# Two F blocks of a SwiGLU down projection: a plain pair, or part of a two-pair Strassen group

## Chip, cores and metric

One Trainium2 chip, one of its cores. The metric is device time in microseconds of one execution, median of three runs before the change.

## The reference

A token block of 2048 x 576 is normalised; a linear-attention branch gives `s`, a SwiGLU feed-forward branch gives `g`, and the result is `x + s * silu(g)`. Cut to what matters here:

```python
def _B_ref(x, w_gate, w_up, w_down):      # F = 4608
    g = _silu(x @ w_gate)
    u = x @ w_up
    return (g * u) @ w_down

xn = _layernorm(x, axis=-1)
s = _A_ref(xn, A_wqkv, A_w_phi, A_wo)     # linear attention, heads of 18
g = _silu(_B_ref(xn, B_w_gate, B_w_up, B_w_down))
return x + s * g
```

So there is a SiLU inside the feed-forward branch (after `w_gate`) and a second one, the gate, on its finished result. The change touches the second.

## The kernel before

**Number format.** Every fp32 operand is split into a high and a low part (`split`, L57: ScalarE copies the high part, VectorE subtracts it to get the low one), and a product is three matmuls: high x high, high x low, low x high (`three`, L665, for the down projection).

**Stages.** Attention first, up to some 500 us. Then the feed-forward branch in two token halves, i = 0 and i = 1, of 1024 tokens each (eight tiles of 128). F is cut into 36 blocks of 128. A *unit* (i, n, f) is one F block f of one half, at place n = 0 to 35 in the half's order (L828 to L833). Six F blocks per half were computed early and lie in DRAM (`stored`, L583); the other units are *gate/up* units (`gate_up`, L591), which multiply the normalised tokens by a block of `w_gate` and `w_up` in a seven-product Strassen scheme and leave h, 128 x 1024, as two tiles `ha` and `hb` of 128 x 512. One product is seven matmuls of 128 x 512 (`product`, L566) into the PSUM tiles px (two buffers), pw and py. Between products ScalarE copies px out (`snap`, L596 to L600) before the next product accumulates into it.

**Down projection.** Two consecutive units make a pair; in pairs, h times `w_down` is a 2 x 2 block product: two token quarters by two F blocks by two column halves of 288. `strassen` (L730) computes it with seven products p1 to p7. Each product has a `prep` (differences on POOL at L753 to L779, then `split_h`, L578, and a split of the 128 x 288 weight block) and two `item`s (L785), each 2 x 3 matmuls of 128 x 288 per pair of the group into one PSUM tile pd (two buffers), followed by one eviction of 128 x 576: a VectorE addition into a running sum at L794 (a ScalarE copy, L792, for the first group of a half). A group normally holds two pairs (four units): the same eviction then serves both pairs. The running sums are `acc[:, 0]` to `acc[:, 3]` (C11, C12, C21, C22), P1 and P6 in the SBUF slot X02, and P7 in `sx`. `combine` (L811), in two parts, adds P1, P6 and P7 into the four C blocks, with POOL and VectorE instructions of 128 x 1152.

36 units are nine times four. Before, the last four units of each half are taken apart: units 32 and 33 are a group of a single pair, then comes `combine`, and units 34 and 35 are a `plain` pair (L672): for each of eight token tiles ScalarE copies the combined `acc` into pd (L690), 24 matmuls add both F blocks of the pair, and the result leaves PSUM. In the first half it leaves through the gate's SiLU back into `acc` (L698) and a 288 KB write to `y_dram`, issued from ScalarE (L699); in the second half `finish` (L637) multiplies it by `s`, adds `x` and writes the output.

**Order.** The down projection's steps go into a Python list, `queue`. `fill` (L846) is called four times in each unit (in a gate/up unit after the second, fourth, fifth and seventh product; four times in a row in a stored unit) and emits items until their cost reaches `share`: 2 up to n = 30, 3 from n = 31 (RUSH). An item costs the number of its pairs, a plain tile 2; `fill` stops when 3 cost units (LAG) or less are left. `look` (L836) runs the prep of the steps soon due. `combine`'s parts are put in ahead of p2 and p3 and behind them (L900 to L903). With the queue's rules followed by hand, the items fall like this around the border between the halves (x2 and x1: pairs in the group; T0 to T7: plain tiles):

```
i=0 n=32  p7 p4 | p4 p5 | p5 p6 | p6 p2   all x2
    n=33  p2 p3 x2 | p3 x2, p1 x1 | - | -
    n=34  p1 p7 p7 | p4 p4 p5 | p5 p6 p6 | combine0 p2   all x1
    n=35  - | - | - | -
i=1 n=0   p2 p3 x1 | p3 x1, combine1, T0 | T1 | T2     (stored)
    n=1   T3 | T4 | T5 | T6
    n=2   - | - | - | -
    n=3   T7 | p1 | p1 | p7   x2, first group of the second half
```

The emitted program is then ordered for each engine by a list scheduler with its own cost model, in which px copies, SiLUs and additions of `gate_up` have high priority; so items may move some way from their call. All engines run their own queue in order. SP issues the loads and stores: at the border seven X tiles of the second half (L514 to L530, each into the slot that the last unit of the first half frees), then the stored h (L586), weights (L546, L555), `w_down` rows (rt, rb at L727; for a plain pair ld at L679) and the loads of `late_finish` (L645), which turns `y_dram` of the first half into output during the second.

Of the kernel before, what the change touches and what calls it, by code (L numbers as in the profile page):

```python
# [11 lines left out]
AF = mybir.ActivationFunctionType  # L12
# [9 lines left out]
HT = HS // P  # L22
NF = F // P
HALF = D // 2
# [22 lines left out]
def gated_hedgehog_kernel(ctx: ExitStack, tc, x, w_qk, w_v, w_phi, wo, w_gu, w_tail, w_down, ident_in, mask_in, out):  # L47
# [5 lines left out]
    nc = tc.nc  # L53
# [3 lines left out]
    def split(hi, lo, src):  # L57
        nc.scalar.copy(hi, src)  # L58
        nc.vector.tensor_sub(lo, src, hi)  # L59
# [17 lines left out]
    y_dram = dram.tile([HT, P, 2, HALF], F32, name="y_dram")  # L77
# [431 lines left out]
    acc = fp.tile([P, 4, HT // 2, HALF], F32, name="acc")  # L509

    def operands(i):

        xo = [None] * 7
        for n in (0, 6, 1, 3, 5, 2, 4):  # L514
            if n < 3:
                j = (0, 1, 3)[n]
                if i:
                    t = xpool.tile([P, 5, BT], F32R, name=f"X0{j}")
                    nc.sync.dma_start(t.bitcast(F32), a_dram[n])
                else:  # L520
                    t = XB[0][j]
                xo[n] = [t[:, c] for c in range(5)]
                continue
            j = n - 3
            t = xpool.tile([P, 5, BT], F32R, name=f"X1{j}")
            nc.sync.dma_start(t.bitcast(F32).rearrange("p c n -> p (c n)"),
                              sum_dram[i, :, j].rearrange("p s c n -> p (s c n)"))
            v = t.rearrange("p c n -> p (c n)").rearrange("p (s c n) -> p s c n", s=4, c=5)
            xo[n] = [v[:, :, c] for c in range(5)]
        return xo  # L530
# [47 lines left out]
    def split_h(src):  # L578
        t = fp.tile([P, 2, BT], F32R, name="hh", bufs=4)
        split(t[:, 0], t[:, 1], src)  # L580
        return t

    def stored(src, fill):  # L583
        h = h_tile()
        for r in range(2):
            nc.sync.dma_start(h[r], src[:, r * BT:(r + 1) * BT])  # L586
        for _ in range(4):
            fill()
        return h
# [47 lines left out]
    def finish(t, k, pd, sx, eng):  # L637
        r0 = HS + t * P
        a = acc[:, t // 4 * 2:t // 4 * 2 + 2, t % 4][:, k]
        nc.scalar.activation(a, pd, AF.Silu)  # L640
        nc.vector.tensor_mul(a, a, halves_of(sx[:, 0])[:, k])  # L641
        eng.tensor_add(a, a, halves_of(sx[:, 1])[:, k])
        nc.sync.dma_start(halves_of(of[r0:r0 + P, :])[:, k], a)

    def late_finish(t):  # L645

        y = fw.tile([P, D], F32, name="ts")
        sx = fw.tile([P, 2, D], F32, name="ld", bufs=2)
        r = slice(t * P, t * P + P)
        nc.sync.dma_start(halves_of(y), y_dram[t])  # L650
        for m, src in enumerate((s_dram, xf)):
            nc.sync.dma_start(sx[:, m], src[r, :])
        nc.vector.tensor_mul(y, y, sx[:, 0])
        nc.vector.tensor_add(y, y, sx[:, 1])
        nc.sync.dma_start(of[r, :], y)

    def final_rows(n):
        name = ("X02", "X00", "X01", "X03")[3 - n]
        t = xpool.tile([P, 2, 2, D], F32, name=name)
        r = slice(HS + 2 * n * P, HS + 2 * n * P + 2 * P)  # L660
        for m, src in enumerate((s_dram, xf)):
            nc.sync.dma_start(t[:, :, m], src[r, :].rearrange("(a p) n -> p a n", p=P))
        return t

    def three(ps, hs, ws, first):  # L665
        for n, (h, w) in enumerate((a, b) for b, a in zip(ws, hs)):
            mm = ((h[0], w[0]), (h[0], w[1]), (h[1], w[0]))
            for m, (l, r) in enumerate(mm):
                nc.tensor.matmul(ps, l, r, start=first and n == 0 and m == 0, stop=n == len(hs) - 1 and m == 2,  # L669
                                 skip_group_check=True)  # L670

    def plain(i, fs, hr, final):  # L672

        ws = []

        def weights():
            raw = fw.tile([P, 2, D], F32, name="ld", bufs=2)
            for n, f in enumerate(fs):
                nc.sync.dma_start(raw[:, n], w_down[f * P:(f + 1) * P, :])  # L679
            for n in range(2):  # L680
                w = fq.tile([P, 2, D], F32R, name="dw", bufs=3)
                split(w[:, 0], w[:, 1], raw[:, n])
                ws.append(w)

        def tile_of(t, hs):
            pd = fps.tile([P, 2, 512], F32, name="pd", bufs=2)
            fine = i == 1 and t == HT // 2 - 1
            c = slice(t % 4 * P, t % 4 * P + P)
            a2 = acc[:, t // 4 * 2:t // 4 * 2 + 2, t % 4]
            nc.scalar.copy(pd[:, :, 0:HALF], a2)  # L690
            for k in range(2):
                n = slice(k * HALF, (k + 1) * HALF)
                three(pd[:, k, 0:HALF], [(h[:, 0, c], h[:, 1, c]) for h in hs], [(w[:, 0, n], w[:, 1, n]) for w in ws],
                      False)
                if fine:
                    finish(t, k, pd[:, k, 0:HALF], final[t // 2][:, t % 2], nc.vector)
            if i == 0:
                nc.scalar.activation(a2, pd[:, :, 0:HALF], AF.Silu)  # L698
                nc.scalar.dma_start(y_dram[t], a2)  # L699
            elif not fine:  # L700
                finish(t, slice(0, 2), pd[:, :, 0:HALF], final[t // 2][:, t % 2], (nc.vector, nc.gpsimd)[t % 2])

        for r in (1, 0) if i else (0, 1):
            hs = []

            def prep(r=r, hs=hs):
                if not ws:
                    weights()
                hs += [split_h(hr[n][r]) for n in range(2)]

            queue.append([2, prep, [(2, lambda t=4 * r + t, hs=hs: tile_of(t, hs)) for t in range(4)]])
# [3 lines left out]
    def pair_sums(i):  # L715
        if (i, 0) not in extra:
            extra[i, 0] = xpool.tile([P, 2, HT // 2, HALF], F32, name="X02")
        return extra[i, 0]

    def last_sum(i):  # L720
        if (i, 1) not in extra:
            extra[i, 1] = fp.tile([P, HT // 2, HALF], F32, name="sx")
        return extra[i, 1]
# [87 lines left out]
    def combine(i, part, final):  # L811
        P1, P6, P7 = pair_sums(i)[:, 0], pair_sums(i)[:, 1], last_sum(i)
        C11, C12, C21, C22 = (acc[:, n] for n in range(4))
        if part == 0:
            nc.vector.tensor_add(P6, P6, P1)
            nc.vector.tensor_add(P7, P7, P6)
            nc.gpsimd.tensor_add(P6, P6, C22)
            nc.vector.tensor_sub(C21, P7, C21)
            nc.vector.tensor_add(C22, C22, P7)
            for k in (3, 2)[0:2 * i]:  # L820
                final[k] = final_rows(k)
        else:
            nc.gpsimd.tensor_add(C11, C11, P1)
            nc.vector.tensor_add(C12, C12, P6)
            for k in (1, 0)[0:2 * i]:
                final[k] = final_rows(k)

# [41 lines left out]
    finals, late = {}, list(range(HT))  # L869
    for i, n, f in units:  # L870
        share[0] = 2 if n < RUSH else 3
        if i == 1 and n == 0:
            xo = operands(1)
        if f >= EARLY:
            w = kept.pop() if i and kept else ready.pop(0)
            if (i, f) == (0, NF - 1):
                kept.append(w)
            if todo and (i, f) != (0, NF - 1):
                ready.append(gate_up_weights(*todo.pop(0)))
        h = stored(h_dram[i, f], fill) if f < EARLY else gate_up(w, xo, fill, (i, f) == (0, EARLY))  # L880
        if n % 2 == 0:
            g = {"f": (f, units[units.index((i, n, f)) + 1][2]), "h": [h]}
            if n % 4 == 0:
                group = []
            if n < NF - 2:
                group.append(g)
        else:
            g["h"].append(h)
        if n >= NF - 2:
            if n % 2:  # L890
                plain(i, g["f"], g["h"], finals)
            continue
        if n >= NF - 4 or n % 4 > 1:
            strassen(i, group, n % 2, n < 4)
        if n % 2 == 0:
            continue
        if i and n >= 15 and late:
            with tc.issue_after(anchor[-1].ins):
                late_finish(late.pop(0))
        if n == NF - 3:  # L900
            for k in range(2):
                queue.insert(len(queue) - 2 + 3 * k,
                             [0, None, [(0, lambda i=i, k=k: combine(i, k, finals))]])  # L903
# [37 lines left out]
```

## Time and profile before

| | |
|---|---|
| median of three runs | 1654.41 us (1653.33 to 1656.06) |
| profiled execution | 1654.66 us, of it span 1652.9 us |
| granted TensorE clock | 0.999 |
| down matmuls (pd, 128 x 288) | 3048 |
| first half's units | from about 546 us to about 1087 us |
| second half's units | from there to about 1593 us, then a tail without gate/up products |
| VectorE, ScalarE, POOL busy | 71%, 43%, 38% of the span |
| DMA queue of SP | 44.9% of the 16 engines' time |

How to read it: a matmul's length in the trace is that of one alone; they overlap, so the distance between the starts of two groups, divided by the count, is the price of one. Idle time of an engine other than TensorE costs nothing unless TensorE ends up waiting. A row of the timeline gives start, length, engine, line, operation, output and input tiles, count, and in brackets idle time before it and what ended that. In the tables of waits the line in front is the waiter.

### The profile page before, as it was taken

To read this page: it belongs to the slowest core of one execution; us is meant where nothing else is said; L and a number is where in the kernel's file an instruction comes from. 1 tells how busy PE (TensorE), PEld (TensorE's weight loads), DVE (VectorE), ACT (ScalarE), POOL (GpSimd) and SP (SyncE) were. 2 spreads that over 40 slices of the span, in tenths; PEclk is the share of its full clock that TensorE was granted. 3 is DMA by queue.
4 is the path that set the end of the run, shared out by engine and by line. 5 is a ranking of instruction groups with operands and counts; after the bars stand their busy time and mean duration, and the time that the engine had idled before them with its cause. 6 is when DMAs were issued, how large, how long until landed. Compare 5 with 4: busy or idle time off the path is not lost.

```text
span 1652.9 us, 25205 instructions
## 1 busy us (share of the span) xinstructions
PE 1614.8 (98%) x9441; PEld 1434.1 (87%) x9441; DVE 1175.4 (71%) x1722; ACT 715.7 (43%) x1389; POOL 622.1 (38%) x660
## 2 busy tenths in 40 slices
PE   6999999999999999999999999999999999999998
PEld 5899998999987688888888888888888888888887
DVE  7678758899852477887787777845567667566578
ACT  5533345444431455445444444445433333433334
POOL 3467500343202444554554453422333234133132
PEclk9999999999999999999999999999999999999999
DMA  8623313343218545445445444495444556556435
GB/s 284 215 77 109 109 34 111 94 141 109 73 47 306 182 159 190 158 167 186 161 171 185 174 173 165 132 355 185 152 137 148 164 182 202 171 178 194 139 114 172
DMA packets 118108, 264.69 MB, mean 160 GB/s; under 512 B 12418, under 2 KB 48386, under 8 KB 116194
## 3 DMA queue, kind: packets, MB, share of 16 engines
q1 hardware_dynamic: 107628, 247.44, 44.9%
q0 software_dynamic: 3072, 11.02, 2.4%
q10 hardware_dynamic: 7286, 4.63, 0.9%
q8 instruction: 74, 1.21, 0.3%
q14 instruction: 48, 0.39, 0.1%
HBM read 164.21 MB, written 98.83 MB: 159 GB/s over the span
## 4 chain that ended last, share of the span: by engine, by line
PE 64%; DVE 3%; DMA 1%; issue 1%; POOL 0%; ACT 0%; SPq 0%; DVEq 0%; POOLq 0%
PE px L570 23%; PE pd L669 22%; PE pw L570 11%; PE py L570 6%; PE pe L92 2%; DVE hh L59 1%; DMA ha<-h_dram 1%; DVE acc L641 0%; DVE dw L59 0%; DVE acc L794 0%; DMA X<-s_dram 0%; DMA rb<-in_B_w_down 0%; DVE w L59 0%; DVE X L794 0%; DVE ha L630 0%
## 5 line engine op out<-in xcount | busy, mean ns | idle before, releaser
L669 PEld LDWEIGHTS pd<-dw,hh 128*128 128x128 f32 x3048 | 430.9, 188 | 31.6 <-DVE dw L59 6.4
L669 PE MATMUL pd<-dw,hh 128*128 128x288 f32 x3048 | 448.0, 297 | 8.4 <-DVE dw L59 4.8
L570 PE MATMUL px<-X,w 128*128 128x512 f32 x1440 | 374.8, 394 | 1.8 <-ACT w L58 1.0
L570 PEld LDWEIGHTS px<-X,w 128*128 128x128 f32 x1440 | 261.4, 188 | 55.9 <-ACT s L599 6.1
L570 PE MATMUL pw<-X,w 128*128 128x512 f32 x720 | 186.7, 394 | 0.0
L570 PEld LDWEIGHTS pw<-X,w 128*128 128x128 f32 x720 | 134.0, 189 | 30.2 <-DVE s L604 0.3
L604 DVE TENSOR_TENSOR s<-pw,s 128x512 f32<-128x512 f32 x120 | 82.8, 690 | 105.2 <-ACT s L599 93.4
L92 PE MATMUL pe<-X,wh 128*128 128x512 f32 (+1 forms) x480 | 152.0, 400 | 1.7 <-POOL X L199 0.7
L794 DVE TENSOR_TENSOR acc<-pd,acc 128x576 f32<-128x576 f32 x128 | 96.1, 752 | 72.2 <-PE pd L669 72.0
L599 ACT COPY s<-px 128x512 f32<-128x512 f32 x120 | 70.3, 586 | 156.4 <-PE px L570 156.3
L59 DVE TENSOR_TENSOR hh<-ha,hh 128x512 fp32r<-128x512 f32 x140 | 110.6, 815 | 23.6 <-ACT hh L58 23.0
L58 ACT CAST hh<-ha 128x512 fp32r<-128x512 f32 x140 | 83.1, 620 | 97.2 <-PE pd L669 79.9
L92 PE MATMUL p<-KVWH,X 128*128 128x288 f32 (+1 forms) x640 | 123.6, 298 | 0.9 <-DVE phi L274 0.9
L92 PEld LDWEIGHTS pe<-X,wh 128*128 128x128 f32 (+1 forms) x480 | 88.5, 189 | 19.7 <-DVE h L120 1.5
L766 POOL TENSOR_TENSOR hb<-hb 128x512 f32<-128x512 f32 x34 | 46.1, 1355 | 152.3 <-DVE hb L626 151.8
L92 PEld LDWEIGHTS p<-KVWH,X 128*128 128x128 f32 (+1 forms) x640 | 100.5, 188 | 1.7 <-issue 1.3
L59 DVE TENSOR_TENSOR w<-ld,w 128x512 fp32r<-128x512 f32 (+1 forms) x90 | 76.3, 848 | 34.2 <-ACT w L58 33.2
L753 POOL TENSOR_TENSOR h<-ha,hb 128x512 f32<-128x512 f32 x34 | 45.7, 1344 | 142.6 <-DVE ha L630 101.1
L570 PE MATMUL px<-X,wt 96*128 96x512 f32 x240 | 94.8, 395 | 0.0
L570 PE MATMUL py<-X,w 128*128 128x512 f32 x360 | 93.7, 394 | 0.1
L58 ACT CAST w<-ld 128x512 fp32r<-128x512 f32 (+1 forms) x90 | 49.4, 549 | 83.5 <-POOL ld L560 50.8
L779 POOL TENSOR_TENSOR ha<-ha 128x512 f32<-128x512 f32 x34 | 52.3, 1554 | 80.5 <-DVE hh L59 80.5
(181 smaller groups left out, 3046.9 us busy)
## 6 DMA issues: line engine op xcount, KB each, us to landing
w_dram<-w SPq DMA_DIRECT2D x87, 512.0 KB, 2.8
w<-w_dram SPq DMA_DIRECT2D x87, 512.0 KB, 4.5
wt<-t_dram SPq DMA_DIRECT2D x59, 336.0 KB, 3.4
ld<-in_B_w_gu SPq DMA_DIRECT2D x30, 512.0 KB, 4.4
X<-sum_dram SPq DMA_DIRECT2D x8, 1280.0 KB, 6.6
rt<-in_B_w_down SPq DMA_DIRECT2D x33, 288.0 KB, 3.2
rb<-in_B_w_down SPq DMA_DIRECT2D x33, 288.0 KB, 3.4
w_dram<-w SPq DMA_DIRECT2D x29, 256.0 KB
```

What stands on the lines that cost most here:

```text
L58: nc.scalar.copy(hi, src)
L59: nc.vector.tensor_sub(lo, src, hi)
L92: nc.tensor.matmul(ps, l, r, start=n == 0, stop=n == len(pairs) - 1)
L570: nc.tensor.matmul(ps, l, r, start=first and n == 0, stop=last and n == len(mm) - 1, skip_group_check=True)
L599: nc.scalar.copy(t, ps)
L604: nc.vector.tensor_add(t, ps, t)
L669: nc.tensor.matmul(ps, l, r, start=first and n == 0 and m == 0, stop=n == len(hs) - 1 and m == 2, skip_group_check=True)
L753: sub(s, g["h"][0][0], g["h"][0][1])
L766: nc.gpsimd.tensor_add(a21, a21, g["h"][1][1])
L779: sub(a12, a12, g["h"][0][0])
L794: nc.vector.tensor_add(a2, pd[:, :, 0:HALF], a2)
```

## The change

In the first half the last four units form one ordinary two-pair group, like the eight groups before it; `plain` stays for the second half only. `combine` of the first half comes after that group, and each of its parts ends with the gate: for each of the two C blocks that it has finished, one SiLU of 128 x 1152 in place on `acc` and one write into `y_dram`, issued from ScalarE (two C blocks hold the same four token tiles, one column half each). The second half's grouping is the same as before.

```diff
--- before.py
+++ after.py
@@ -669,7 +669,7 @@
                 nc.tensor.matmul(ps, l, r, start=first and n == 0 and m == 0, stop=n == len(hs) - 1 and m == 2,
                                  skip_group_check=True)
 
-    def plain(i, fs, hr, final):
+    def plain(fs, hr, final):
 
         ws = []
 
@@ -684,7 +684,7 @@
 
         def tile_of(t, hs):
             pd = fps.tile([P, 2, 512], F32, name="pd", bufs=2)
-            fine = i == 1 and t == HT // 2 - 1
+            fine = t == HT // 2 - 1
             c = slice(t % 4 * P, t % 4 * P + P)
             a2 = acc[:, t // 4 * 2:t // 4 * 2 + 2, t % 4]
             nc.scalar.copy(pd[:, :, 0:HALF], a2)
@@ -694,13 +694,10 @@
                       False)
                 if fine:
                     finish(t, k, pd[:, k, 0:HALF], final[t // 2][:, t % 2], nc.vector)
-            if i == 0:
-                nc.scalar.activation(a2, pd[:, :, 0:HALF], AF.Silu)
-                nc.scalar.dma_start(y_dram[t], a2)
-            elif not fine:
+            if not fine:
                 finish(t, slice(0, 2), pd[:, :, 0:HALF], final[t // 2][:, t % 2], (nc.vector, nc.gpsimd)[t % 2])
 
-        for r in (1, 0) if i else (0, 1):
+        for r in (1, 0):
             hs = []
 
             def prep(r=r, hs=hs):
@@ -811,17 +808,28 @@
     def combine(i, part, final):
         P1, P6, P7 = pair_sums(i)[:, 0], pair_sums(i)[:, 1], last_sum(i)
         C11, C12, C21, C22 = (acc[:, n] for n in range(4))
+
+        def gate(*ns):
+            for n in ns:
+                nc.scalar.activation(acc[:, n], acc[:, n], AF.Silu)
+                r = slice(n // 2 * 4, n // 2 * 4 + 4)
+                nc.scalar.dma_start(y_dram[r, :, n % 2].rearrange("t p n -> p t n"), acc[:, n])
+
         if part == 0:
             nc.vector.tensor_add(P6, P6, P1)
             nc.vector.tensor_add(P7, P7, P6)
             nc.gpsimd.tensor_add(P6, P6, C22)
             nc.vector.tensor_sub(C21, P7, C21)
             nc.vector.tensor_add(C22, C22, P7)
+            if i == 0:
+                gate(2, 3)
             for k in (3, 2)[0:2 * i]:
                 final[k] = final_rows(k)
         else:
             nc.gpsimd.tensor_add(C11, C11, P1)
             nc.vector.tensor_add(C12, C12, P6)
+            if i == 0:
+                gate(0, 1)
             for k in (1, 0)[0:2 * i]:
                 final[k] = final_rows(k)
 
@@ -882,22 +890,22 @@
             g = {"f": (f, units[units.index((i, n, f)) + 1][2]), "h": [h]}
             if n % 4 == 0:
                 group = []
-            if n < NF - 2:
+            if i == 0 or n < NF - 2:
                 group.append(g)
         else:
             g["h"].append(h)
-        if n >= NF - 2:
+        if i and n >= NF - 2:
             if n % 2:
-                plain(i, g["f"], g["h"], finals)
+                plain(g["f"], g["h"], finals)
             continue
-        if n >= NF - 4 or n % 4 > 1:
+        if n % 4 > 1 or (i and n >= NF - 4):
             strassen(i, group, n % 2, n < 4)
         if n % 2 == 0:
             continue
         if i and n >= 15 and late:
             with tc.issue_after(anchor[-1].ins):
                 late_finish(late.pop(0))
-        if n == NF - 3:
+        if n == (NF - 1, NF - 3)[i]:
             for k in range(2):
                 queue.insert(len(queue) - 2 + 3 * k,
                              [0, None, [(0, lambda i=i, k=k: combine(i, k, finals))]])
```

With the same rules of the queue the items fall so (all x2):

```
i=0 n=32  p7 p4 | p4 p5 | p5 p6 | p6 p2
    n=33  p2 p3 | - | - | -
    n=34  - | - | - | -
    n=35  p3 p1 | p1 p7 | - | -
i=1 n=0   p7 | p4 | p4 | p5     (stored)
    n=1   p5 | p6 | p6 | combine0 with its gate, p2
    n=2   p2 | p3 | - | -
    n=3   p3 | combine1 with its gate, p1 | p1 | p7     (from p1 on: first group of the second half)
```

## The prediction

> **What bounds the kernel now.** I read the page first: the busy shares, the chain that ended last, and the largest groups.
>
> ```profile
> span 1652.9 us, 25205 instructions
> PE 1614.8 (98%) x9441; PEld 1434.1 (87%) x9441; DVE 1175.4 (71%) x1722; ACT 715.7 (43%) x1389; POOL 622.1 (38%) x660
> PE px L570 23%; PE pd L669 22%; PE pw L570 11%; PE py L570 6%; PE pe L92 2%; DVE hh L59 1%; DMA ha<-h_dram 1%; DVE acc L641 0%; DVE dw L59 0%; DVE acc L794 0%; DMA X<-s_dram 0%; DMA rb<-in_B_w_down 0%; DVE w L59 0%; DVE X L794 0%; DVE ha L630 0%
> ```
>
> TensorE ends nearly everything: gate and up products (px, pw, py) and down products (pd). An average over the span says nothing of the place of the change, so I cut windows: a period of four gate/up units in the first half, the stretch around the border between the halves, a period of the second half. Columns: PE, PEld, DVE, ACT, POOL busy with instruction counts, clock, DMA share, GB/s.
>
> ```profile
> 920.25:988.12 67.87, 67.87 (x366) 59.38 (x365) 50.73 (x75) 32.29 (x64) 33.09 (x33) 1.00 0.50 176
> 988.12:1136.48 148.36, 147.91 (x798) 128.59 (x797) 98.95 (x142) 69.78 (x133) 49.99 (x44) 1.00 0.62 217
> 1136.64:1193.11 56.47, 56.47 (x317) 50.08 (x317) 29.93 (x42) 28.07 (x56) 17.89 (x17) 1.00 0.49 147
> ```
>
> In all three PE is busy to within 0.5 us, and the clock is 1.00. So the first term is a count of matmuls, and everything else acts only by making PE wait. "Busy" can hide bubbles, so I take the price of a matmul from the distance between starts in a full stretch.
>
> ```profile
> 1025.27 3.38 PE L669 MATMUL pd<-dw,hh 128*128 128x288 f32 x24
> 1028.49 1.55 PE L570 MATMUL px<-X,w 128*128 128x512 f32 x6
> 1029.87 0.40 PE L570 MATMUL px<-X,wt 96*128 96x512 f32 x1
> 1030.10 1.09 PE L570 MATMUL pw<-X,w 128*128 128x512 f32 x4
> ...
> L669 PE MATMUL pd<-dw,hh 128*128 128x288 f32 x385 | 57.2, 297 | 0.4 <-DVE X L794 0.4
> ```
>
> 24 down matmuls take 1028.49 - 1025.27 = 3.22 us, 0.134 us each (not the 0.297 us that a single one lasts); a gate/up product of 7 takes 1.61 us, 0.230 us each. The last row is the border stretch: 385 of its 798 matmuls are down matmuls. 385 x 0.134 + 413 x 0.230 = 146.6 us, against 148.36: all bubbles around the border come to 1.8 us. That is the ceiling for anything gained beyond the matmuls.
>
> **Matmuls removed: -1.6 us.** A plain pair costs 8 tiles x 2 column halves x 2 F blocks x 3 = 96 matmuls. A group of one pair costs 7 products x 2 items x 2 x 3 = 84, a group of two pairs 7 x 2 x 2 x 2 x 3 = 168. 96 + 84 becomes 168: 12 fewer, 12 x 0.134 = 1.61 us.
>
> **One wait removed: -0.45 us.** With one pair, an item is 6 matmuls, 0.8 us, and its DVE eviction takes as long; here PE had to wait.
>
> ```profile
> 1056.80 0.39 PE L570 MATMUL py<-X,w 128*128 128x512 f32 x1
> 1057.63 1.06 PE L669 MATMUL pd<-dw,hh 128*128 128x288 f32 x6 [0.45 <-DVE X L794]
> L794 DVE TENSOR_TENSOR acc<-pd,acc 128x576 f32<-128x576 f32 x128 | 96.1, 752 | 72.2 <-PE pd L669 72.0
> ```
>
> Two-pair items are 1.6 us against the same 0.75 us, as in the period at 920, which has no gap. Bounds: -0.45 to 0 (another late eviction in its place). I take -0.45. The other 1.3 us of bubbles I leave as they are; bounds -1.3 to 0.
>
> **Items moved: +0.8 us.** By the code's own counting (2 cost units to a call of `fill`, 3 from n = 31 on, 3 held back), before, unit 34 was filled by ten one-pair items and unit 35 by none, and the plain tiles stood in units 0 and 1 of the second half. After, part 0 of the joint group is queued only at the end of unit 34: the last three calls of unit 33 and all four of unit 34 find only the one item held back. A call stands where PE would otherwise wait for ScalarE to copy px out:
>
> ```profile
> 1078.62 0.97 PE L669 MATMUL pd<-dw,hh 128*128 128x288 f32 x6
> 1079.45 1.66 PE L570 MATMUL px<-X,w 128*128 128x512 f32 x6
> 1078.82 0.59 ACT L599 COPY s<-px 128x512 f32<-128x512 f32 x1 [1.03 <-PE px L570]
> ...
> 563.87 0.30 PE L669 MATMUL pd<-dw,hh 128*128 128x288 f32 x1
> 564.70 1.66 PE L570 MATMUL px<-X,w 128*128 128x512 f32 x6 [0.54 <-ACT s L599]
> ```
>
> The hole is 0.83 us: six matmuls fill it at 1078.62; with one matmul, early in the first half, 0.54 us of idle PE is left. Units 33 and 34 have four such holes and one item of 12 matmuls, enough for two. The other two can take matmuls of the next unit's first product (px has two buffers). Bounds 0 to 2 x 0.83 = 1.7; I take the middle, 0.8.
>
> **Added on ACT, DVE and POOL: 0, while they have room.**
>
> ```profile
> L58 ACT CAST hh<-ha 128x512 fp32r<-128x512 f32 x140 | 83.1, 620 | 97.2 <-PE pd L669 79.9 <-POOL ha L779 12.7 <-DVE ha L630 3.6
> L59 DVE TENSOR_TENSOR hh<-ha,hh 128x512 fp32r<-128x512 f32 x140 | 110.6, 815 | 23.6 <-ACT hh L58 23.0 <-PE px L570 0.4
> L58 ACT CAST dw<-td 128x288 fp32r<-128x288 f32 x102 | 40.2, 430 | 4.9 <-PE pd L669 2.8 <-POOL td L754 1.5 <-POOL td L761 0.6
> L59 DVE TENSOR_TENSOR dw<-td,dw 128x288 fp32r<-128x288 f32 x102 | 62.6, 637 | 0.9 <-ACT dw L58 0.9
> 1069.01 0.67 ACT L58 CAST dw<-ld 128x576 fp32r<-128x576 f32 x1 [1.91 <-PE pd L669]
> 1069.71 0.76 DVE L59 TENSOR_TENSOR dw<-ld,dw 128x576 fp32r<-128x576 f32 x1
> L690 ACT COPY pd<-acc 128x576 f32<-128x576 f32 x16 | 10.2, 642 | 3.2 <-ACT acc L698 1.8 <-DVE acc L824 1.1
> L698 ACT ACTIVATE acc<-pd 128x576 f32<-128x576 f32 x8 | 5.2, 651 | 4.7 <-PE pd L669 4.7
> 1093.71 0.59 ACTq L699 DMA_DIRECT2D y_dram<-acc  x1
> y_dram<-acc ACTq DMA_DIRECT2D x8, 288.0 KB, 5.5
> ```
>
> h splits go from 11 to 14, half weight splits from 7 to 14, whole ones from 2 to 0. DVE: 3 x 0.815 + 7 x 0.637 - 2 x 0.76 = +5.4 us; evictions into the sums stay at 14. ACT: 3 x 0.62 + 7 x 0.43 - 2 x 0.67 = +3.5; eight copies into PSUM and eight SiLUs go (8 x 1.29 = -10.3) and four SiLUs of 1152 elements come. None of that size is in the trace; each lies between one of 576 (0.65) and two (1.30); I take 1.3, so +5.2. Eight issues become four. ACT ends 1.6 us lighter, without counting four issues fewer.
>
> POOL gets the second pair's differences of weight blocks (128x288) and of h (128x512):
>
> ```profile
> L754 POOL TENSOR_TENSOR td<-rb,rt 128x288 f32<-128x288 f32 x33 | 34.0, 1030 | 78.3 <-DMA rb<-in_B_w_down 78.3
> L779 POOL TENSOR_TENSOR ha<-ha 128x512 f32<-128x512 f32 x34 | 52.3, 1554 | 80.5 <-DVE hh L59 80.5
> ```
>
> The smaller kind comes four times (L754, L759, L760, L761), the larger four times (L753, L766, L771, L779): 4 x 1.03 + 4 x 1.55 = at most 10.3 us. The period at 920 carries a joint group's whole load and weight splits besides, with DVE at 51 and POOL at 33 of 68 us and PE without a gap; in the second half DVE has 30 of 56. That room is the cover. Without it, an eviction that is late by its own 0.75 us stalls PE by as much once both pd buffers are full. In bytes the DMAs are unchanged: two w_down rows come through rt and rb instead of ld, ahead of the X loads on SP; y_dram gets its eight 288 KB as four writes.
>
> The SiLU now waits for combine: behind each on ACT stand its DMA issue (0.59) and then px copies. Two in a row hold ACT for 2 x (1.3 + 0.59) = 3.8 us; a px copy caught behind costs PE up to that less the hole's 0.83 (+3.0). Before, eight copy-SiLU-issue sets of 1.9 us stood among px copies with PE fully busy, so I take 0; bounds 0 to +3.0.
>
> **Sum.** -1.6 - 0.45 + 0.8 = -1.25 us. The profiled execution took 1654.66 us (its span and 1.8 around it), 0.25 over the median 1654.41. Set against the median: 1653.1. Own range, by the bounds of the holes, the wait and the bubbles: 1651.0 to 1654.5 (the bubbles all gone, the holes all open with the wait back).
>
> **Rivals.** *Everything closes up.* If the new order leaves no bubble at all, 1.6 + 1.8 = 3.4 us go: 1651.0. For it: second-half groups run gapless (row at 1136.64). Against: seven empty calls.
>
> *It gives back what it saves.* At that upper end, -1.6 + 1.7, nothing is won: 1654.5.
>
> *POOL stands behind a late transfer: slower.*
>
> ```profile
> 1081.99 3.12 POOL L823 TENSOR_TENSOR acc<-acc,X 128x1152 f32<-128x1152 f32 x1 [3.83 <-DVE acc L794]
> 1105.36 1.29 POOL L753 TENSOR_TENSOR h<-ha,hb 128x512 f32<-128x512 f32 x1 [20.24 <-DMA hb<-h_dram]
> 1073.97 0.33 SPq L519 DMA_DIRECT2D X<-a_dram  x1
> X<-sum_dram SPq DMA_DIRECT2D x8, 1280.0 KB, 6.6
> 1094.36:1115.24 20.88, 20.88 (x118) 18.51 (x117) 3.42 (x5) 10.73 (x18) 3.87 (x3) 1.00 0.94 306
> ```
>
> POOL sat 20 us at L753, the second half's first difference, for the stored hb. SP loads seven X tiles of 1280 KB from 1073.97 on, 9 MB, 29 us at 306 GB/s, and hb comes behind them. Behind L753 stood only work of its own group; after, the joint group's P6 and P3 (L771, L779) may stand there. 78 fewer down matmuls ahead of unit 35 bring the X loads 10.5 us forward, to about 1063, and hb to about 1095. P6's first item is due about 31 us after these loads begin (six products of unit 35 and four of the next gate/up unit, 16.1 us, and nine items, 14.5), at 1093 to 1094, and needs two L771 and a split, some 5 us before. If L753 was placed ahead, P6 is ready at 1100 or later: some +7 us, about 1660. It decides only if L753 stands before L771. Against it: earlier in program order is P6.
>
> *DVE stands behind combine: slower.*
>
> ```profile
> 1073.45 1.95 DVE L816 TENSOR_TENSOR sx<-sx,X 128x1152 f32<-128x1152 f32 x1
> 1075.99 3.38 DVE L818 TENSOR_TENSOR acc<-sx,acc 128x1152 f32<-128x1152 f32 x1
> 1079.30 1.34 DVE L819 TENSOR_TENSOR acc<-acc,sx 128x1152 f32<-128x1152 f32 x1
> L815 DVE TENSOR_TENSOR X<-X 128x1152 f32<-128x1152 f32 x2 | 2.7, 1352 | 0.0
> ```
>
> L818 took 3.38 us against 1.34 for L819 of the same size. Combine's DVE chain, 8.0 us with L815's 1.35, now falls among two-pair items and their POOL work. If two evictions wait it out, pd covers 3.2 us and PE loses up to 4.8: 1658. Against: at 1073 it ran among items with PE busy. The Trainium skill, "SBUF — State Buffer" (section "SBUF: two separate sides"), says VectorE with two SBUF inputs and GpSimd lock each other out of a shared port for a whole instruction; L818 agrees. By that rule alone the added POOL work could delay DVE by all its 10 us; the gapless period at 920 speaks against that reaching PE.
>
> **How the numbers follow.** Forecast 0.44, closing up 0.22, giving back 0.10, POOL 0.17, DVE 0.07. The time is the forecast's, 1653.1. About 0.2% (3.3 us: below 1651.1 or above 1657.7) is what a measurement here tells from no change. Of closing up, 0.15 lies beyond it; POOL and 0.06 of DVE lie beyond it on the other side: faster 0.15, same 0.62, slower 0.23. The range 1650.6 to 1658.0 leaves out POOL's case and a tail of closing up.
>
> **What would show it.** Down matmuls 3048 to 3036, each step still 0.134 us; no wait for L794 near 1057; idle PE behind ACT s L599 in units 33 and 34 of at most 1.7 us; four SiLUs of about 1.3 us; L753 after L771 and L779 on POOL. PE waiting for hh or dw right after the border, with POOL idle on hb, would make me wrong.

## Result, and the profile after

| | before | after |
|---|---|---|
| median, ten runs each | 1653.82 us | 1658.57 us |
| lowest to highest | 1651.75 to 1656.06 | 1656.94 to 1661.0 |
| ratio after / before, 95% interval | | 1.0031 [1.0022, 1.0039] |
| profiled execution, span | 1654.66, 1652.9 us | 1659.47, 1657.7 us |

The change makes the kernel slower by 0.3%, 4.75 us between the medians. (Lines of `strassen` and `combine` have moved: L794 is now L791, L753 is L750, L771 is L768. New are L814, the SiLU of the gate, L816, its write, L819 to L823 for combine's first part, L829 and L830 for its second.)

First the page of the kernel after: total, busy shares, and two of its groups.

```profile
span 1657.7 us, 25181 instructions
PE 1616.3 (98%) x9429; PEld 1435.2 (87%) x9429; DVE 1181.0 (71%) x1730; ACT 712.9 (43%) x1385; POOL 631.4 (38%) x668
L669 PE MATMUL pd<-dw,hh 128*128 128x288 f32 x3036 | 447.7, 298 | 7.3 <-DVE dw L59 4.0
L570 PE MATMUL px<-X,w 128*128 128x512 f32 x1440 | 375.4, 394 | 4.4 <-ACT s L599 3.4
```

The 12 matmuls are gone (3048 to 3036), VectorE has 5.6 us more (1175.4 to 1181.0), ScalarE 2.8 less, POOL 9.3 more, close to what was counted. What is new is idle time in front of the px products: 4.4 us in the whole run against 1.8. The stages say where; the same windows of the kernel after, columns as in the prediction:

```profile
920.25:988.12 67.87, 67.87 (x366) 59.40 (x366) 50.73 (x74) 32.28 (x64) 33.09 (x34) 1.00 0.51 178
988.12:1136.48 148.36, 143.37 (x765) 123.42 (x764) 104.11 (x146) 63.84 (x122) 62.64 (x52) 1.00 0.60 210
1136.64:1193.11 56.47, 56.47 (x317) 50.07 (x317) 29.25 (x41) 28.60 (x57) 17.86 (x16) 1.00 0.52 160
```

On either side of the border TensorE is as full as before; at the border it is 5.0 us idle (148.36 - 143.37), where it had been 0.45. (The window holds 765 matmuls instead of 798, because all that follows comes later by what was lost.) The table of TensorE's waits from 988.12 to 1141.2 names three (total, times, longest):

```profile
PE px L570 <- ACT s L599: 2.5, 1, 2.5
PE py L570 <- ACT py L611: 1.3, 1, 1.3
PE pw L570 <- DVE s L604: 1.1, 1, 1.1
```

Three single waits, 4.9 us. Less the 1.6 us of the 12 matmuls and the 0.45 us of idle before, +2.9 us. Between two corresponding places, the py product of unit 33 (1041.38 us before, 1041.91 after) and the last pw product of the second half's unit 3 (1134.86 and 1139.55), 4.2 us are lost in all; the rest is small gaps of 0.1 us, most of them in the units left empty. Of the 4.8 us between the two profiled executions another 0.5 lie ahead of unit 33, in work that the change leaves alone; most of that comes between 605 and 615 us, where the granted clock of the second fell as low as 0.74 while that of the first did not fall. Each wait has an instruction in front of it on an engine that works in order. The first, unit 34, from the timelines of TensorE, ScalarE and POOL:

```profile
1056.79 1.66 PE L570 MATMUL py<-X,w 128*128 128x512 f32 x6 [1.28 <-ACT py L611]
...
1055.84 0.40 ACT L58 CAST w<-ld 128x256 fp32r<-128x256 f32 x1 [3.09 <-POOL ld L560]
1056.15 0.58 ACT L611 COPY py<-px 128x512 f32<-128x512 f32 x1
...
1052.13 1.29 POOL L763 TENSOR_TENSOR hb<-hb 128x512 f32<-128x512 f32 x1 [3.87 <-DVE hb L626]
1053.50 1.62 POOL L768 TENSOR_TENSOR ha<-hb,ha 128x512 f32<-128x512 f32 x1
1055.09 0.72 POOL L560 TENSOR_TENSOR ld<-ld,ts 128x256 f32<-128x256 f32 x1
```

Read from the bottom: L560, a difference for the next unit's weights, stands behind a sum and a difference for the joint group (L763, L768) on POOL; the cast of its result stands in front of L611 on ScalarE; py waits for L611. With units 33 and 34 nearly empty of down products, TensorE reaches this place sooner than the order of the other engines provides for. The second and third, at combine, in the second half's unit 2:

```profile
1118.61 1.65 PE L570 MATMUL px<-X,w 128*128 128x512 f32 x6 [2.54 <-ACT s L599]
1124.15 1.67 PE L570 MATMUL pw<-X,w 128*128 128x512 f32 x6 [1.09 <-DVE s L604]
...
1110.98 1.17 ACT L814 ACTIVATE acc<-acc 128x1152 f32<-128x1152 f32 x1 [2.33 <-DVE acc L822]
1116.92 1.16 ACT L814 ACTIVATE acc<-acc 128x1152 f32<-128x1152 f32 x1 [4.26 <-DVE acc L823]
1117.99 0.57 ACT L599 COPY s<-px 128x512 f32<-128x512 f32 x1
...
1115.53 1.36 DVE L823 TENSOR_TENSOR acc<-acc,sx 128x1152 f32<-128x1152 f32 x1 [4.58 <-POOL X L821]
1118.07 4.40 DVE L59 TENSOR_TENSOR dw<-rt,dw 128x288 fp32r<-128x288 f32 x2
1123.42 0.68 DVE L604 TENSOR_TENSOR s<-pw,s 128x512 f32<-128x512 f32 x1
...
1112.82 2.67 POOL L821 TENSOR_TENSOR X<-X,acc 128x1152 f32<-128x1152 f32 x1
1117.63 3.03 POOL L829 TENSOR_TENSOR acc<-acc,X 128x1152 f32<-128x1152 f32 x1 [2.14 <-DVE acc L791]
1120.62 1.53 POOL L768 TENSOR_TENSOR ha<-hb,ha 128x512 f32<-128x512 f32 x1
```

L821 adds the old C22 into P6, so L823, which overwrites C22, must wait for it. L821 could have run when L820 ended on VectorE at 1109.0 (in e7 below it waits for just that), but stood behind L757 and L763 in POOL's queue until 1112.82; the SiLU of C22 waits for L823 at the head of ScalarE's queue, and the px copy L599 behind it is what TensorE needs. Then two weight splits take 4.40 us (at 1077 and 1078 two of the same take 0.45 each) while L829 and L768 run on POOL, and L604 comes late.

### The profile page after: what moved, and what is told of

Read it like the earlier page. It is cut to its first block, busy times and chain, and to the rows that moved or that the text cites. A ratio compares the mean times of both kernels' runs of the same rounds, so it can differ in the third digit from the quotient of the medians.

```text
span 1657.7 us, 25181 instructions
## 1 busy us (share of the span) xinstructions
PE 1616.3 (98%) x9429; PEld 1435.2 (87%) x9429; DVE 1181.0 (71%) x1730; ACT 712.9 (43%) x1385; POOL 631.4 (38%) x668
## 5 line engine op out<-in xcount | busy, mean ns | idle before, releaser
L791 DVE TENSOR_TENSOR acc<-pd,acc 128x576 f32<-128x576 f32 x128 | 96.0, 751 | 75.8 <-PE pd L669 75.7
L604 DVE TENSOR_TENSOR s<-pw,s 128x512 f32<-128x512 f32 x120 | 82.7, 689 | 90.3 <-ACT s L599 77.0
L599 ACT COPY s<-px 128x512 f32<-128x512 f32 x120 | 70.2, 585 | 160.7 <-PE px L570 160.6
L763 POOL TENSOR_TENSOR hb<-hb 128x512 f32<-128x512 f32 x35 | 46.8, 1337 | 167.9 <-DVE hb L626 167.5
L750 POOL TENSOR_TENSOR h<-ha,hb 128x512 f32<-128x512 f32 x35 | 47.0, 1342 | 123.8 <-DVE ha L630 103.7
L776 POOL TENSOR_TENSOR ha<-ha 128x512 f32<-128x512 f32 x35 | 53.8, 1554 | 85.8 <-DVE hh L59 85.8
```

The costliest lines, as they stand in the source:

```text
L599: nc.scalar.copy(t, ps)
L604: nc.vector.tensor_add(t, ps, t)
L750: sub(s, g["h"][0][0], g["h"][0][1])
L763: nc.gpsimd.tensor_add(a21, a21, g["h"][1][1])
L776: sub(a12, a12, g["h"][0][0])
L791: nc.vector.tensor_add(a2, pd[:, :, 0:HALF], a2)
```

## Experiments

The theory: three in-order waits, separate and additive. The main rival: the stretch is bound by the X loads or by the total work, and time freed in one place is lost again. Each kernel was timed against the kernel before on the same chip, in 4 to 11 executions.

**e1: the first wait alone.** In `gate_up_weights` (L560):

```diff
-            nc.gpsimd.tensor_sub(ld[:, 1], ld[:, 1], ts[:, 1])
+            (nc.vector if f >= NF - 2 else nc.gpsimd).tensor_sub(ld[:, 1], ld[:, 1], ts[:, 1])
```

> The last two F blocks' final weight difference (L560) is computed on VectorE, in the first half, so that in unit 34 ScalarE's copy L611 no longer stands behind a cast that waits for POOL; TensorE's order is the same as after the change. Theory 'three in-order waits' (TensorE lost 1.28 us behind L611, 2.54 us behind L599, 1.09 us behind L604, and these add): some 1.3 us less than after the change, 1657.2, ratio to before 1.002; the wait of py for L611 at 1056.8 is gone and the other two stay as long as they were. Rival 'the time comes back': the stretch around the border is bound by the burst of X loads or by the total work of POOL and VectorE, so that what is freed here is lost further on: 1658.5, ratio 1.003.

Measured 1657.52 us, ratio 1.0020 [1.0011, 1.0030]. TensorE's waits at the border in its trace, and its timeline at that wait:

```profile
PE px L570 <- ACT s L599: 2.4, 1, 2.4
...
1117.08 2.21 PE L570 MATMUL px<-X,w 128*128 128x512 f32 x6 [2.38 <-ACT s L599]
1119.09 0.63 PE L570 MATMUL px<-X,wt 96*128 96x512 f32 x1
1119.51 3.32 PE L570 MATMUL px<-X,w 128*128 128x512 f32 x10
```

The wait for L611 is gone and 1.1 us of the median with it. The wait for L604 is not in the table either, but its time was lost in another way. Behind the wait for L599 the matmuls ran slower, the single one 0.63 us instead of 0.40; the granted clock is 0.71 from 1117.08 to 1119.10 us and 0.68 from there to 1122.60. The 17 matmuls took 1.7 us more than at 0.230 each, and L604 was done at 1122.53, before TensorE needed it. So the expectation that the other two waits stay holds for L599 alone.

**e2: the second wait alone.** In `combine`:

```diff
-            nc.gpsimd.tensor_add(P6, P6, C22)
+            (nc.gpsimd if i else nc.vector).tensor_add(P6, P6, C22)
```

> combine's addition of C22 into P6 (L821) is done on VectorE instead of POOL in the first half, so that C22 and its SiLU do not wait for POOL's queue. Three in-order waits: L823 then follows L822 at once, the second SiLU L814 no longer holds ScalarE for 4.3 us, and TensorE's wait for L599 (2.54 us) goes; the wait for L604 may stay (1.09 us): 1656.1, ratio 1.0014. Rival 'the SiLUs themselves': what hurts is the length of four SiLUs of 1.17 us in front of px copies, not what they wait for; then at most 1 us is won: 1657.6 or more. Rival 'the time comes back': 1658.5.

Measured 1655.53 us, ratio 1.0009 [1.0000, 1.0018]: 3.0 us less. The waits, and ScalarE's timeline at the place:

```profile
PE pw L570 <- DVE s L604: 1.6, 1, 1.6
PE py L570 <- ACT py L611: 1.3, 1, 1.3
```

```profile
1113.16 1.17 ACT L814 ACTIVATE acc<-acc 128x1152 f32<-128x1152 f32 x1 [0.99 <-DVE acc L822]
...
1114.80 0.59 ACT L599 COPY s<-px 128x512 f32<-128x512 f32 x1 [0.15 <-PE px L570]
1115.53 1.17 ACT L814 ACTIVATE acc<-acc 128x1152 f32<-128x1152 f32 x1
```

The SiLUs are as long as before, 1.17 us, and cost nothing now: the second waits for nobody, and the px copy has come in front of it. What hurt was a SiLU that waits, not a SiLU.

**e3: both additions on VectorE.** As e2, and the same for `tensor_add(C11, C11, P1)`.

> Both POOL additions of the first half's combine (L821 into P6 and L829 into C11) are done on VectorE. Three in-order waits: the wait for L599 goes (2.54 us), and the one for L604 (1.09 us) as well, if the weight splits in front of it were slow (4.40 us for two) because POOL worked at the same time: 1655.0, ratio 1.0007. If VectorE was simply full there, the 1.35 us added to it makes the wait for L604 longer: 1656.5 or more, and the two splits still take some 4 us.

Measured 1655.04 us, ratio 1.0008 [0.9999, 1.0017]. The median is the expected one, the mechanism only half:

```profile
1116.42 1.90 DVE L59 TENSOR_TENSOR dw<-rt,dw 128x288 fp32r<-128x288 f32 x2
1118.25 0.81 DVE L59 TENSOR_TENSOR dw<-td,dw 128x288 fp32r<-128x288 f32 x2
1118.98 1.96 DVE L829 TENSOR_TENSOR acc<-acc,X 128x1152 f32<-128x1152 f32 x1
1120.87 0.74 DVE L791 TENSOR_TENSOR acc<-pd,acc 128x576 f32<-128x576 f32 x1
1121.53 0.67 DVE L604 TENSOR_TENSOR s<-pw,s 128x512 f32<-128x512 f32 x1
```

The two splits fell from 4.40 to 1.90 us with L829 off POOL (in e2, with L829 still there, they took 4.40), so POOL had held them; but the 1.96 us of L829 now stand in front of L604, and the wait for it is still 1.0 us. From e2 to e3 the intervals overlap; no gain of its own is shown for the second addition.

**e4: e1 and e3 together.**

> The edits of the two kernels before it together: L560 of the last two F blocks and both POOL additions of combine on VectorE. Three in-order waits: all three go, 4.9 us, 1653.7, ratio to before 1.000: the 12 matmuls saved are then paid for by the small bubbles in the empty units 33 and 34. Rival 'the time comes back': 1657 or more.

Measured 1653.92 us, ratio 0.9999 [0.9990, 1.0008]; of the waits, 0.6 us for L604 is left. e1 took 1.1 us off the median, e3 3.5, both 4.7: they add, and the rival "the time comes back" falls. With the waits taken away, the joint group is where the kernel before was, not yet faster.

**e5 and e6: is it the SiLU or what it waits for?** e5 takes the SiLU out of combine and applies it in `late_finish`; e6 issues the writes from SP besides.

```diff
-        nc.vector.tensor_mul(y, y, sx[:, 0])
+        nc.scalar.activation(y, y, AF.Silu); nc.vector.tensor_mul(y, y, sx[:, 0])
...
-                nc.scalar.activation(acc[:, n], acc[:, n], AF.Silu)
```

> The four SiLUs leave combine; late_finish applies the SiLU to each token tile (eight of 128x576) when it reads y_dram. The writes into y_dram stay on ScalarE, where each still has to wait for its C block. In-order waits (what holds ScalarE is the wait for C22, not the length of the SiLU): ScalarE stands at the second write until C22 is there, px copies behind it, TensorE's wait at that place stays 2 us or more: 1658.0, ratio 1.0025. Rival 'the SiLUs themselves': without 4 x 1.17 us in front of px copies the wait goes: 1656.0, ratio 1.0013.

> As the kernel before it, but the four writes into y_dram are issued from SP: ScalarE has nothing of combine left. In-order waits: TensorE's wait for L599 goes (2.54 us), those for L611 (1.28) and L604 (1.1 to 1.6) stay: 1656.0, ratio 1.0013. If SP then stands at the writes in front of weight loads, TensorE waits for weights instead: 1658 or more.

Measured 1666.65 us (1.0070 [1.0058, 1.0083]) and 1669.1 us (1.0090 [1.0075, 1.0104]): both expected times were missed by far. At the border e5 behaves as the theory has it. ScalarE's timeline in e5, there and later (ACTq: DMA issues):

```profile
1109.97 6.29 ACTq L816 DMA_DIRECT2D y_dram<-acc  x2
1116.31 0.58 ACT L615 ACTIVATE py<-py 128x512 f32<-128x512 f32 x1 [8.67 <-DVE acc L823]
1348.77 0.68 ACT L653 ACTIVATE ts<-ts 128x576 f32<-128x576 f32 x1 [4.13 <-DMA ts<-y_dram]
1349.36 0.57 ACT L599 COPY s<-px 128x512 f32<-128x512 f32 x1
```

A write that waits holds ScalarE as a SiLU does: 6.29 us for two issues, and TensorE's wait for L599 is 2.9 us with no SiLU there at all. Most of the rest of the loss is a wait that the edit brought: L653 stands in front of px copies and waits for y_dram's load, 19.2 us in eight times; TensorE waits another 6.3 us for L599 in the second half (5.2 in e6). The slow matmuls seen in e1 come too: behind two of e5's waits (2.9 us at the border, 2.8 at 1349.98), and behind the longest of e6, where the granted clock is 0.56 from 1123.24 to 1130.00 us and 2.8 us are lost. In e6 the wait for L599 is gone from the border, but the weight splits still take 4.37 us beside POOL, and L604 comes 4.1 us late:

```profile
1114.28 1.36 DVE L823 TENSOR_TENSOR acc<-acc,sx 128x1152 f32<-128x1152 f32 x1 [3.81 <-POOL X L821]
1116.82 4.37 DVE L59 TENSOR_TENSOR dw<-rt,dw 128x288 fp32r<-128x288 f32 x2
1122.51 0.67 DVE L604 TENSOR_TENSOR s<-pw,s 128x512 f32<-128x512 f32 x1
```

With L821 left in POOL's queue, taking the SiLU out of combine moved the loss at the border, to the write or to L604, and did not end it.

**e7: fill the empty units.** In the unit loop:

```diff
-        share[0] = 2 if n < RUSH else 3
+        share[0] = 2 if i == 0 or n < RUSH else 3
```

> The first half keeps 2 cost units a call to its end (3 from n = 31 on in the second half alone): the joint group's predecessor is spread over units 31 to 34, and units 33 and 34 have two empty calls instead of seven. If the empty units let TensorE run ahead of POOL's weight difference, the wait for L611 goes with them, and so do some small bubbles of 0.1 us: 1.3 to 1.9 us less, 1656.9, ratio 1.0019, with the waits for L599 and L604 unchanged. If the wait for L611 comes from the order on ScalarE and POOL alone, it stays: 1658.5.

Measured 1655.09 us, ratio 1.0004 [0.9996, 1.0013]: 3.5 us less than after the change, more than expected. The waits at the border:

```profile
PE pw L570 <- DVE s L604: 1.0, 1, 1.0
PE px L570 <- ACT s L599: 1.0, 1, 1.0
```

The wait for L611 and the small gaps are gone, as expected. That the one for L599 fell from 2.5 to 1.0 was not; POOL's order is another here, with L821 ahead of the second pair's weight differences:

```profile
1101.36 1.29 POOL L763 TENSOR_TENSOR hb<-hb 128x512 f32<-128x512 f32 x1
1103.94 2.67 POOL L821 TENSOR_TENSOR X<-X,acc 128x1152 f32<-128x1152 f32 x1 [1.30 <-DVE sx L820]
1106.57 1.93 POOL L751 TENSOR_TENSOR td<-rb,rt 128x288 f32<-128x288 f32 x1
```

It waits 1.3 us for its operand now instead of standing behind the weight differences of both pairs.

**e8: e7 and e3 together.**

> Spread items (as in the kernel before it) together with both POOL additions of combine on VectorE. In-order waits, additive: 1658.6 - 1.6 - 3.5 = 1653.5, ratio 0.9997; at best, with all bubbles but those of the kernel before the change gone, 1652.3. Rival: the two edits share what they free, and it stays near the 1655.0 of combine on VectorE alone.

Measured 1652.54 us, ratio 0.9991 [0.9982, 0.9999]. That is near the best case named, 1652.3. One wait is left, 1.0 us for L604.

**e9, control: e7's line in the kernel before the change.**

> Control: the kernel before the change with nothing but the spread items in the first half (2 cost units a call to its end), still with the group of one pair and the plain pair. If spreading is worth its 3.5 us only because the joint group left seven calls empty, the kernel before gains nothing, its gaps around the border being 1.7 us in all: 1653.0 to 1655.0, ratio 0.9994 to 1.0005. If spreading helps any tail of the first half, 1652.5 or less, ratio 0.999, and the joint group has no merit of its own in the fastest version.

Measured 1657.59 us, ratio 1.0017 [1.0008, 1.0026]: neither; it loses 2.9 us. Its waits at the border:

```profile
PE pw L570 <- DVE s L604: 2.0, 1, 2.0
PE pd L669 <- DVE acc L794: 1.4, 1, 1.4
PE py L570 <- ACT py L611: 0.4, 1, 0.4
```

The waits come to 3.8 us, against 0.45 in the kernel before; behind the longest the granted clock is 0.64 from 1098.18 to 1102.90 us, where 24 down matmuls take 1.5 us more than at 0.134 each. So in these runs the faster pace at the end suits the single pair and the plain tiles, and the slower one the joint group. Grouping and pace belong together, and the gain in e7 is not one that any tail would have had.

**e10: the last wait.** e8, with the addition into C11 queued on VectorE behind the `ha` (L630) of the latest unit:

```diff
-            (nc.gpsimd if i else nc.vector).tensor_add(C11, C11, P1)
+            with ExitStack() if i else tc.issue_after(anchor[-1].ins): (nc.gpsimd if i else nc.vector).tensor_add(C11, C11, P1)
```

> Spread items and combine on VectorE, and the addition into C11 (L829, 1.96 us) made to stand behind the additions of unit 2 of the second half on VectorE instead of in front of its L604. In-order waits: the last wait left at the border (pw for L604, 1.03 us) goes: 1.0 us less than the 1652.5 of the same kernel without this, 1651.5, ratio 0.9985. If VectorE is simply behind by then, the wait moves to the next instruction that needs it and the time stays at 1652.5.

Measured 1652.37 us, ratio 0.9986 [0.9977, 0.9995], 2.4 us less than the 1654.74 of the kernel before, timed beside it. The border and the period behind it:

```profile
988.12:1136.48 148.36, 148.36 (x810) 130.40 (x808) 111.14 (x154) 69.21 (x132) 58.46 (x51) 1.00 0.64 218
1136.48:1193.11 56.63, 56.58 (x315) 49.99 (x315) 31.35 (x45) 27.27 (x55) 18.02 (x16) 1.00 0.53 160
```

TensorE is not idle at the border at all, and this version is 0.14% faster than the kernel before (interval 0.05% to 0.23%). Against e8 the ratios' intervals overlap.

**All traces side by side.** A median also holds what happens far from the border: the py product that starts at 557.58 us before starts between 554.6 and 558.6 us in the other traces. So here is the length of one stretch around the border in each trace, from the py product at 915.24 us to the one at 1223.64 us before, and from and to the same two products elsewhere.

| | stretch, us | less the 308.40 of before |
|---|---|---|
| after | 312.56 | +4.2 |
| e1, first wait | 310.99 | +2.6 |
| e2, second wait | 310.17 | +1.8 |
| e3, both additions | 309.47 | +1.1 |
| e4, e1 and e3 | 308.45 | +0.1 |
| e5, e6, SiLU late | 313.99, 316.36 | +5.6, +8.0 |
| e7, spread | 307.98 | -0.4 |
| e8, e7 and e3 | 306.75 | -1.7 |
| e9, spread before | 313.36 | +5.0 |
| e10, last wait | 305.72 | -2.7 |

Against after, e1 and e3 take 1.6 and 3.1 us off this stretch and e4 4.1. e7 takes 4.6 and e3 3.1, but e8 only 5.8: these two share part of what they free, since each shortens the wait for L599. A trace is one execution, and a drop of the clock is in it or not (1.7 us of e1's stretch, 1.5 of e9's, whose median lies only 2.9 us above before); e7's, at 1652.45 us, is the second fastest of its eleven.

## Why the prediction was wrong

- *Matmuls removed, -1.6 us*: right. 3036 of them, and the price of one is unchanged (24 of them take 1029.01 - 1025.80 = 3.21 us after, 3.22 before). Nothing else in the sum was as safe.
- *One wait removed, -0.45 us*: right; no wait for an eviction is left at the border.
- *Items moved, +0.8 us (bounds 0 to 1.7)*: too small, and not as thought. The holes behind px copies were closed by the next unit's product, at 0.1 us each (nine small gaps in units 33 and 34, some 0.9 us, against two before); another 1.28 us came from L611, behind a cast that waited for POOL, and e1 and e7 both remove that. Together some 2 us, beyond the upper bound.
- *Added on ACT, DVE and POOL: 0, while they have room*: this is the step that failed. ScalarE's part was given bounds of 0 to +3.0 and 0 was taken, because eight sets of copy, SiLU and issue had stood among px copies without harm; the upper end of 1654.5 left the +3.0 out. But those SiLUs waited for TensorE's own matmuls; the new one waits for a chain over VectorE and POOL, and cost 2.54 us. For VectorE and POOL the busy share of a window was taken for cover (51 and 33 of 68 us), and the only price named for them in this step was a late eviction; none was late. e2 shows how little it says: the same amount of work, one instruction moved off POOL's queue, and the wait is gone. L604's 1.09 us belong to this step too: 3.63 us where the sum has 0.
- *The rivals.* POOL behind the stored hb did not occur: L750 stands behind L768 and L776 in the order, the condition that the text named for it not to count. DVE behind combine was the nearest, with 0.07 and 4.8 us: the lock between POOL and VectorE did delay the splits, but two of the three waits are elsewhere. None of the cases had several covers fail at once, so the range ended at 1658.0, below the 1658.57 measured.
- Together, -1.6 - 0.45 + 1.28 + 2.54 + 1.09 = +2.9 us, and small gaps bring it to the 4.2 us measured at the border.

What stays open: why e9's order has these waits was not followed; what decides whether the clock falls behind a wait, no run here shows; and some shift of order with every edit may be worth a few tenths of a microsecond either way.

## What to carry to other kernels

Where TensorE is full, a saving of matmuls is safe and small, and it is paid for wherever work that it displaces is put at the head of an in-order queue. Idle shares of an engine are no cover: look, for every instruction that is moved, at what it waits for and which instruction behind it the busiest engine needs next. Here a long chain across engines (VectorE, POOL, VectorE, ScalarE) did best with its additions on one engine and the last of them behind the urgent instructions, not between them.

## What the runs showed of the hardware

How hard POOL and VectorE hold each other up was more than expected. Two splits of 128x288, 0.45 us each elsewhere, took 4.40 us while L829 (3.03 us) and L768 (1.53) ran on POOL, and 1.90 us when L829 was not there (e3). This agrees with the lock that "SBUF — State Buffer" of the Trainium skill describes in the section "SBUF: two separate sides": the first split takes 2.91 us and ends at 1120.98, after L829 (1120.66), the second takes 1.56 and ends at 1122.47, after L768 (1122.15). A DMA issue on ScalarE that has to wait holds the engine as a computation does (6.29 us for two issues in e5).

A wait of TensorE can cost more than its length. Behind waits of 2.4 us (e1), 2.9 and 2.8 (e5), 4.1 (e6) and 2.0 (e9) its granted clock was between 0.50 and 0.71 for some 3 to 7 us, 1.5 to 2.8 us lost each time; behind the 2.54 us in the trace of the kernel after it was 1.00.
